# Four head pairs turned by rows at the start, gate rows before ranks, list scans set apart, and the last rows stored in column pieces

## The chip, the core and the metric

The kernel is one program on one core of one Trainium2 chip. The metric is its device time in microseconds (us). Times of single executions come from the hardware profiler; its lines name the engines as PE (TensorE matmul), PEld (TensorE weight load), DVE (VectorE), ACT (ScalarE), POOL (GpSimd) and SP (SyncE, which mostly issues transfers). A line such as L573 is a line of the kernel's file.

## What is computed

Sigmoid attention over 8 batches of 12 heads (448 tokens, head size 64), whose output rows are the 3584 tokens of a top-1 mixture of 8 experts (768 to 1024 to 768):

```python
scores = scale * np.matmul(q, k.transpose(0, 1, 3, 2)) - np.log(S)      # scale = 1/8, S = 448
attn_out = np.matmul(1.0 / (1.0 + np.exp(-scores)), v)
x = attn_out.transpose(0, 2, 1, 3).reshape(B * S, H * D)                # 3584 x 768
logits = x @ w_gate
expert_idx = np.argmax(logits, axis=1)
probs = softmax(logits)                                                 # with 1e-9 in the divisor
gate_w = probs[np.arange(N), expert_idx]
for e in range(E):
    xe = x[expert_idx == e]
    out[expert_idx == e] = gate_w[...] * (np.maximum(xe @ w1[e], 0.0) @ w2[e])
```

All inputs and the output are float32. The matmuls of the experts are made of three passes over numbers split into a high and a low part (`w1h`, `w1l`, `xh`, `xl`, `hh`, `hl`), those of the attention run in float32, where one matmul of the program shows as two records in the profile.

## The kernel before

**Attention.** Two heads of a batch are a pair g; there are 48 pairs, taken two at a time. A pair's keys and queries (`kn`, `qn`, loaded by `load_pair`) are needed with the head dimension on the partitions (`kt`, `qt`). For g < `BY_ROWS` they are loaded by rows and turned by small matmuls against the identity (`turn`, L534), head h in the diagonal quarter `OWN[h]` of the 128x128 array, first all of k, then all of q, and a copy moves the turned tile from PSUM to SBUF (L537: k by DVE, q by ACT). For all other pairs four transfers each bring 32-column pieces and DVE turns them (`nc.vector.transpose`). The keys of a pair come in seven chunks, called steps, 168 in all. `scores(s)` makes four 64x64x448 matmuls (two pairs, two heads) that lie in the four quarters of the array (L573); `squash` is the sigmoid on ACT (L558); `weighted(s)` makes the four matmuls with v (L589). A score tile is one of a ring of four PSUM buffers (`ps_sc`), which the small gate tiles (`pr`, `pg`) share. `ps_moe` is a ring of two PSUM buffers for everything else at the start and for the experts' sums, `ps_av` holds the sums with v.

**Order.** Nothing of this is left to a scheduler: the stretch is written under `manual_schedule`, and every engine works through its instructions in the order in which the code emits them. The steps before `START` = 70 are attention alone. From step 70 on, a generator `mo` of the experts' matmuls (`moe`, L213 the first layer, L236 the second) is mixed in: `more(7)` twice per step (`MIX`). A first-layer sum is followed by ACT's `hh` (L220) and DVE's `hl` (L221), a second-layer tile by DVE's L248 (times the gate row `gt`) and L249 (transpose into `ob`, which SP stores). POOL makes the low parts of the weights (L133, `w1l` and `w2l`), each after ACT has made the high part.

**Gate.** For each batch the routing is worked out in stages that the tables `EARLY`, `FIRST_LATE`, `LATE` and `LAST` put at steps of a 21-step period (PB; entry r, r = 14 is the first step of a group of seven, i = 0). Of these, `c3` (L344 to L350) makes `gates` on DVE; `d` (`gate_d`) makes two PE matmuls `pr` (L360, L361) and on DVE the chain `pre`, `base`, `rk`, `sl`, `si` (L364 to L375), the position of each token in its expert's list; `d2` scatters records by it; `g` (`gate_g`) makes `nw` and, in two instructions, `gs` on DVE (L402, L404, L405); `e` (`gate_e`) makes four PE transposes `pg` of `gs` (L413) and ACT copies them to `gt` (L415). In the tables before, `d` comes at r = 14, `g` and `d2` at r = 16, `e` at r = 17. At r = 14 a stage is emitted between the seven expert matmuls of the step before and the next four score tiles.

**Start.** `warm_up(WARM)` sends 34 matmuls on constants to PE while the first transfers run. Then the transfers and turns of pairs 0 and 1 follow; between the first score tiles of pair 0 and of pair 1 twelve more such matmuls stand (`FILL`).

**End.** When attention is over, the tokens that the first pass did not cover are worked off in items of 256 rows. The lists of items come from two scans on DVE over `w2s` (`tensor_tensor_scan`, L801), then `ends` (L803, L804) and other small steps, with `more(24)` twice among them. The last two items are straight-line code (`large`, second layer L914 and L921, result rows `xo`), and POOL scatters their rows into `out` by indirect transfers (`scatter`, L850, 128 rows of 3 KB each); the last of these scatters is the program's last work.

## Time and profile before

| | |
|---|---|
| median of three runs | 800.8 us (800.42 to 801.74) |
| the profiled execution | 803.83 us, its span 801.9 us |
| mean granted TensorE clock | 0.997 of full speed |
| PE busy | 789.7 us, 98% of the span |
| PEld busy | 613.6 us, 77% |
| ACT, POOL, DVE busy | 391.2, 360.3 and 355.1 us, 49%, 45% and 44% |
| transferred | 124.09 MB, mean 155 GB/s |

The span runs from the first to the last instruction; what lies around it in the profiled execution is 1.9 us. A timeline row reads: start, busy time, engine, line, operation, tile written <- tiles read, elements, count, and in brackets how long the engine had been idle and what released it. An instruction's time on PE overlaps that of its neighbours, since four matmuls in four quarters of the array run at once.

### The profile page before, as it was taken

How to read it: one execution, taken by the hardware profiler on the slowest of the kernel's cores; microseconds unless marked ns; L12 is line 12 of the kernel's file. 1: busy time of each engine (PE TensorE's matmuls, PEld its weight loads, DVE VectorE, ACT ScalarE, POOL GpSimd, SP SyncE). 2: the span in 40 equal slices, each digit the busy share in tenths (PEclk: the TensorE clock that was granted, in tenths of full speed). 3: DMA queues.
4: the chain of work that ended last, by engine and by line, in shares of the span. 5: the costliest groups of instructions: out<-in, count | busy, mean ns of one | idle time of the engine just before them, and what ended most of it. 6: DMA issues, size and time to landing. Idle time of an engine off the chain costs nothing. (4 is left out here: it accounts for less than half of the span.)

```text
span 801.9 us, 15879 instructions
## 1 busy us (share of the span) xinstructions
PE 789.7 (98%) x5726; PEld 613.6 (77%) x5726; DVE 355.1 (44%) x787; ACT 391.2 (49%) x711; POOL 360.3 (45%) x346
## 2 busy tenths in 40 slices
PE   9999999999999999999999999999999999999996
PEld 6655555777787778766777678777788998999996
DVE  2344456462535435362443525355267174334443
ACT  5877777454533554454544545355342342335342
POOL 8658665353223424243242334233553664574350
PEclk9999999999999999999999999999999999999998
DMA  9997998895669937489575874747166445556671
GB/s 178 157 180 129 169 218 183 181 214 110 145 136 200 197 74 166 114 189 183 106 168 99 195 173 113 182 123 182 50 162 169 138 134 158 162 135 176 190 216 38
DMA packets 312372, 124.09 MB, mean 155 GB/s; under 512 B 209502, under 2 KB 309934, under 8 KB 312288
## 3 DMA queue, kind: packets, MB, share of 16 engines
q1 hardware_dynamic: 305920, 110.80, 63.1%
q0 software_dynamic: 6048, 11.76, 6.1%
q8 instruction: 47, 0.77, 0.4%
q10 hardware_dynamic: 320, 0.46, 0.2%
q14 instruction: 37, 0.30, 0.1%
HBM read 100.89 MB, written 22.47 MB: 154 GB/s over the span
## 5 line engine op out<-in xcount | busy, mean ns | idle before, releaser
L558 ACT ACTIVATE at<-sc,bias_s 128x448 f32<-128x448 f32 x336 | 188.2, 640 | 114.2 <-PE sc L573 111.8
L133 POOL TENSOR_TENSOR w1l<-wst,w1h 128x768 fp32r<-128x768 f32 x72 | 132.3, 1846 | 206.5 <-ACT w1h L132 197.4
L133 POOL TENSOR_TENSOR w2l<-wst,w2h 128x512 fp32r<-128x512 f32 x84 | 107.0, 1294 | 155.5 <-ACT w2h L132 155.5
L573 PE MATMUL sc<-qt,kt 64*64 64x448 f32 x1344 | 171.2, 549 | 1.0 <-ACT at L558 0.7
L589 PE MATMUL av<-at,vn 64*64 64x448 f32 x1344 | 167.0, 539 | 0.8 <-ACT at L558 0.7
L573 PEld LDWEIGHTS sc<-qt,kt 64*64 64x64 f32 x1344 | 87.1, 192 | 54.6 <-issue 31.5
L213 PE MATMUL ps<-xh,w1h 128*128 128x448 f32 x336 | 124.2, 370 | 1.8 <-DVE w2s L809 1.3
L213 PE MATMUL ps<-xl,w1h 128*128 128x448 f32 x336 | 123.6, 368 | 0.0
L213 PE MATMUL ps<-xh,w1l 128*128 128x448 f32 x336 | 123.6, 368 | 0.0
L236 PE MATMUL ps<-hh,w2h 128*128 128x448 f32 x336 | 123.3, 367 | 0.0
L236 PE MATMUL ps<-hl,w2h 128*128 128x448 f32 x336 | 123.3, 367 | 0.0
L236 PE MATMUL ps<-hh,w2l 128*128 128x448 f32 x336 | 123.1, 366 | 0.0
L589 PEld LDWEIGHTS av<-at,vn 64*64 64x64 f32 x1344 | 63.4, 133 | 60.1 <-issue 42.2
L132 ACT CAST w2h<-wst 128x512 fp32r<-128x512 f32 x108 | 65.2, 622 | 57.3 <-PE ps L236 43.9
L220 ACT ACTIVATE hh<-ps 128x448 fp32r<-128x448 f32 x56 | 30.6, 547 | 123.3 <-PE ps L213 121.6
L221 DVE SCALAR_TENSOR_TENSOR hl<-ps,hh 128x448 fp32r<-128x448 f32 x56 | 34.8, 621 | 119.8 <-ACT hh L220 113.5
L248 DVE TENSOR_TENSOR ps<-ps,gt 128x448 f32<-128x448 f32 x42 | 26.4, 629 | 136.0 <-PE ps L236 135.9
L213 PEld LDWEIGHTS ps<-xh,w1h 128*128 128x128 f32 x336 | 63.1, 188 | 11.5 <-issue 4.5
L236 PEld LDWEIGHTS ps<-hh,w2h 128*128 128x128 f32 x336 | 65.2, 194 | 7.1 <-issue 3.5
L236 PEld LDWEIGHTS ps<-hl,w2h 128*128 128x128 f32 x336 | 65.2, 194 | 6.6 <-issue 3.7
L236 PEld LDWEIGHTS ps<-hh,w2l 128*128 128x128 f32 x336 | 65.2, 194 | 5.9 <-issue 2.8
L213 PEld LDWEIGHTS ps<-xl,w1h 128*128 128x128 f32 x336 | 63.1, 188 | 8.7 <-issue 3.5
(160 smaller groups left out, 945.3 us busy)
## 6 DMA issues: line engine op xcount, KB each, us to landing
wst<-in_moe_w_dram SPq DMA_DIRECT2D x72, 384.0 KB
wst<-in_moe_w_dram SPq DMA_DIRECT2D x54, 512.0 KB
x_tok<-xt SPq DMA_DIRECT2D x64, 168.0 KB
qn<-in_q_dram SPq DMA_DIRECT2D x184, 56.0 KB
raw<-x_tok SPq DMA_DIRECT2D x28, 336.0 KB
out_dram<-ob SPq DMA_DIRECT2D x84, 112.0 KB
vn<-in_v_dram SPq DMA_DIRECT2D x60, 112.0 KB
kn<-in_k_dram SPq DMA_DIRECT2D x104, 56.0 KB
```

Of the source, the lines that this page charges most:

```text
L132: nc.scalar.copy(hi, st)
L133: eng.tensor_tensor(lo, st, hi.bitcast(F32), op=ALU.subtract)
L213: nc.tensor.matmul(ps[:, :S], a[:, ws], b_, start=(t == 0 and n == 0), stop=(t == KD - 1 and n == 2))
L220: nc.scalar.activation(hh[:, :S], ps[:, :S], AF.Relu)
L221: nc.vector.scalar_tensor_tensor(hl[:, :S], ps[:, :S], 0.0, hh[:, :S].bitcast(F32), op0=ALU.max, op1=ALU.subtract)
L236: nc.tensor.matmul(ps[:, :S], a, b_, start=(j == 0 and n == 0), stop=(j == KF - 1 and n == 2))
L248: nc.vector.tensor_tensor(ps[:, :S], ps[:, :S], gate_rows[b], op=ALU.mult)
L558: nc.scalar.activation(at, ps[:, :S], AF.Sigmoid, bias=bias_s, scale=SCALE)
L573: nc.tensor.matmul(ps[quarter(g, h), :S], ks, ops[g, "q"][OWN[h]], start=True, stop=True)
L589: nc.tensor.matmul(psv[g][OWN[h], :S], ops[g, "v"][rows, c, :], at[rows], start=(c == 0), stop=(c == KC - 1))
```

## The change

Four edits, in the order of the program:

1. **Start.** `BY_ROWS` goes from 2 to 4, and a new `turn_rows(g)` turns keys and queries of a pair together, chunk by chunk: k in the two diagonal quarters of the array, q in the other two (its heads are loaded into the swapped halves). Pairs 0 and 1 are turned ahead of the scores; pair 2 after the score tiles of steps 0 and 1 and pair 3 after those of steps 2 and 3, by `READY` at u = 0 (before, DVE turned them). The copies of the first two pairs are split: DVE takes the first chunk of k, ACT four chunks of q, DVE the other three, then the rest of k. k of a pair comes in one transfer by SP, v of an even pair in one transfer. The transfers of pairs 2 and 3 are issued ahead of the turns. The twelve `FILL` matmuls go, `WARM` is 30 instead of 34.
2. **Gate.** In `LATE` and `FIRST_LATE` (five of the eight batches) `g` moves to r = 13, `e` to r = 14, `d` to r = 17, `d2` to r = 19.
3. **Scans.** Twelve expert matmuls are emitted after each of the two scans.
4. **Last rows.** Of the last 128 rows, two thirds of the columns are scattered by two early indirect transfers of 1 KB pieces, with row numbers `at_d` made by three small DVE instructions; the last scatter carries the remaining third.

```diff
@@ -493,11 +493,13 @@
             return
         b, hp = divmod(g, NP)
         if g < BY_ROWS:
-            for nm, src, eng in (("k", k, nc.sync), ("q", q, nc.scalar)):
-                t = apool.tile([P, KC, D], F32, tag=nm + "n", bufs=4, name=f"{nm}n_{g}")
-                for h in range(2):
-                    eng.dma_start(t[OWN[h]], src[b, 2 * hp + h].rearrange("(p c) d -> p c d", c=KC))
-                ops[g, nm + "n"] = t
+            t = apool.tile([P, KC, D], F32, tag="kn", bufs=4, name=f"kn_{g}")
+            nc.sync.dma_start(t, k[b, 2 * hp : 2 * hp + 2].rearrange("h (p c) d -> (h p) c d", c=KC))
+            ops[g, "kn"] = t
+            t = apool.tile([P, KC, D], F32, tag="qn", bufs=4, name=f"qn_{g}")
+            for h in range(2):
+                nc.scalar.dma_start(t[OWN[1 - h]], q[b, 2 * hp + h].rearrange("(p c) d -> p c d", c=KC))
+            ops[g, "qn"] = t
             return
@@ -516,8 +518,12 @@
             return
         b, hp = divmod(g, NP)
         t = apool.tile([P, KC, D], F32, tag="vn", bufs=4, name=f"vn_{g}")
+        eng = nc.scalar if g == 0 else nc.gpsimd if 4 <= g < K_POOL else nc.sync
+        if g % 2 == 0:
+            eng.dma_start(t, v[b, 2 * hp : 2 * hp + 2].rearrange("h (p c) d -> (h p) c d", c=KC))
+            ops[g, "v"] = t
+            return
         for h in range(2):
-            eng = nc.gpsimd if 4 <= g < K_POOL else nc.sync
             eng.dma_start(t[quarter(g, h)], v[b, 2 * hp + h].rearrange("(p c) d -> p c d", c=KC))
         ops[g, "v"] = t
@@ -526,21 +532,33 @@
         if g >= NG:
             return
         t = apool.tile([P, S], F32, tag=nm + "t", bufs=4, name=f"{nm}t_{g}")
-        if g < BY_ROWS:
-            rows = ops.pop((g, nm + "n"))
-            ps = ps_moe.tile([P, 512], F32, tag="moe", name=f"turn_{nm}_{g}")
-            for c in range(KC):
-                for own in OWN:
-                    nc.tensor.matmul(
-                        ps[own, c * DK : (c + 1) * DK], rows[own, c, :], ident[own, own], start=True, stop=True
-                    )
-            (nc.vector.tensor_copy if nm == "k" else nc.scalar.copy)(
-                t.rearrange("d (p c) -> d c p", c=KC), ps[:, :S].rearrange("d (c p) -> d c p", c=KC)
-            )
-            ops[g, nm] = t
-            return
         nc.vector.transpose(t, ops.pop((g, nm + "n")).rearrange("p j s -> p (j s)"))
         ops[g, nm] = t
+
+    def turn_rows(g):
+
+        rows = [ops.pop((g, x + "n")) for x in "kq"]
+        pool, tag = (ps_av, "av") if g == 1 else (ps_moe, "moe")
+        pk, pq = (pool.tile([P, 512], F32, tag=tag, name=f"turn_{x}_{g}") for x in "kq")
+        for c in range(KC):
+            for n, ps in enumerate((pk, pq)):
+                for h in range(2):
+                    at = OWN[h if n == 0 else 1 - h]
+                    nc.tensor.matmul(
+                        ps[OWN[h], c * DK : (c + 1) * DK], rows[n][at, c], ident[at, at], start=True, stop=True
+                    )
+        kt, qt = (apool.tile([P, S], F32, tag=f"{x}t", bufs=4, name=f"{x}t_{g}") for x in "kq")
+        q_to = qt.rearrange("d (p c) -> d c p", c=KC)
+        q_at = pq[:, :S].rearrange("d (c p) -> d c p", c=KC)
+        if g < 2:
+            nc.vector.tensor_copy(kt[:, :DK], pk[:, :DK])
+            nc.scalar.copy(q_to[:, :4], q_at[:, :4])
+            nc.vector.tensor_copy(q_to[:, 4:], q_at[:, 4:])
+            nc.vector.tensor_copy(kt[:, DK:], pk[:, DK:S])
+        else:
+            nc.vector.tensor_copy(kt, pk[:, :S])
+            nc.vector.tensor_copy(q_to, q_at)
+        ops[g, "k"], ops[g, "q"] = kt, qt
 
     def warm_up(n):
@@ -566,10 +584,9 @@
         two = [2 * u + n for n in range(2)]
         pss = [score_tile(f"{g}_{c}") for g in two]
         for g, ps in zip(two, pss):
-            if s == 0 and g == 1:
-                warm_up(FILL)
+            by = "d (c p) -> d c p" if g < BY_ROWS else "d (p c) -> d c p"
             for h in range(2):
-                ks = ops[g, "k"][OWN[h]].rearrange("d (p c) -> d c p", c=KC)[:, c]
+                ks = ops[g, "k"][OWN[h]].rearrange(by, c=KC)[:, c]
                 nc.tensor.matmul(ps[quarter(g, h), :S], ks, ops[g, "q"][OWN[h]], start=True, stop=True)
         for g, ps in zip(two, pss):
@@ -598,7 +615,7 @@
-    WARM, FILL, K_POOL, BY_ROWS = 34, 12, 22, 2
+    WARM, K_POOL, BY_ROWS = 30, 22, 4
@@ -607,10 +624,10 @@
     MIX = (7, 7)
 
     READY = {
-        0: lambda u: (turn(2 * u + 2, "k"), load_pair(2 * u + 4)),
-        1: lambda u: (turn(2 * u + 2, "q"), load_values(2 * u + 2)),
-        3: lambda u: (turn(2 * u + 3, "k"), load_pair(2 * u + 5)),
-        4: lambda u: (turn(2 * u + 3, "q"), load_values(2 * u + 3)),
+        0: lambda u: (turn(2 * u + 2, "k") if u else turn_rows(2), load_pair(2 * u + 4)),
+        1: lambda u: (turn(2 * u + 2, "q") if u else None, load_values(2 * u + 2)),
+        3: lambda u: (turn(2 * u + 3, "k") if u else turn_rows(3), load_pair(2 * u + 5)),
+        4: lambda u: (turn(2 * u + 3, "q") if u else None, load_values(2 * u + 3)),
     }
 
@@ -621,16 +638,17 @@
         warm_up(WARM)
         load_pair(0)
         load_pair(1)
-        for g in range(2):
-            turn(g, "k")
-            turn(g, "q")
-            load_values(g)
+        load_values(0)
+        load_values(1)
+        load_pair(2)
+        load_pair(3)
+        turn_rows(0)
+        turn_rows(1)
         nc.gpsimd.memset(wg, 0.0)
         nc.gpsimd.dma_start(wg[:, :, :E], w_gate.rearrange("(t p) e -> p t e", p=P))
         setup()
-        for g in (2, 3):
-            load_pair(g)
-            load_values(g)
+        load_values(2)
+        load_values(3)
         done_av = done_sc = 0
@@ -668,10 +686,10 @@
             elif what == "e" and b > 0:
                 gate_e(b - 1, g["gs"])
 
-        LATE = {7: "b", 10: "c", 11: ("l", "c2"), 12: "c3", 14: "d", 16: ("d2", "g"), 17: "e"}
+        LATE = {7: "b", 10: "c", 11: ("l", "c2"), 12: "c3", 13: "g", 14: "e", 17: "d", 19: "d2"}
         LAST = {3: "b", 5: "c", 6: ("l", "c2"), 7: "c3", 8: "d", 9: ("d2", "g"), 10: "e"}
         EARLY = {5: "b", 7: ("c", "c2"), 9: ("l", "c3"), 11: "d", 13: ("d2", "g"), 17: "e"}
-        FIRST_LATE = {5: "b", 10: "c", 11: ("l", "c2"), 12: "c3", 14: "d", 16: ("d2", "g"), 17: "e"}
+        FIRST_LATE = {5: "b", 10: "c", 11: ("l", "c2"), 12: "c3", 13: "g", 14: "e", 17: "d", 19: "d2"}
         PLACES = {}
         for b in range(B):
@@ -799,6 +817,7 @@
     until(330)
     for msk, cum in zip((big, few), rank):
         nc.vector.tensor_tensor_scan(cum, cut(3), msk, 0.0, op0=ALU.mult, op1=ALU.add)
+        more(12)
     ends = rest.tile([P, 1], F32, name="ends")
     nc.vector.tensor_scalar(ends, rank[1][:, NI - 1 : NI], 1.0, None, op0=ALU.add)
@@ -846,13 +865,13 @@
             oob_is_err=False,
         )
 
-    def scatter(frm, idx):
+    def scatter(frm, idx, to=out):
         return nc.gpsimd.indirect_dma_start(
-            out=out,
+            out=to,
             out_offset=bass.IndirectOffsetOnAxis(ap=idx, axis=0),
             in_=frm,
             in_offset=None,
-            bounds_check=NT - 1,
+            bounds_check=to.shape[0] - 1,
             oob_is_err=False,
         )
@@ -924,9 +943,18 @@
     def put_rows(xo, h, rec, puts):
         apart(scatter(xo[h], rec[:, h, 0:1]), puts)
 
+    out_d = out.rearrange("n (d f) -> (n d) f", f=DW)
+    at_d = rest.tile([P, ND], U32, name="at_d")
+
+    def put_part(xo, d, puts):
+        apart(scatter(xo[:, d * DW : (d + 1) * DW], at_d[:, d : d + 1], out_d), puts)
+
+    outs = {}
+
     def by_stores(h):
         two = opool.tile([P, S // 32, 32, 2], F32, tag="ob", name=f"xo_{h}")
-        return two.rearrange("p j s t -> p (j s t)")
+        outs[h] = two.rearrange("p j s t -> p (j s t)")
+        return outs[h]
 
     def by_hidden(h):
@@ -1052,6 +1080,13 @@
     run(item, 2)
     for h in range(2):
         put_rows(xo, h, recs_2[0], puts)
+    for d in range(ND):
+        nc.vector.tensor_scalar(
+            at_d[:, d : d + 1], recs_2[1][:, 1, 0:1], float(ND), float(d), op0=ALU.mult, op1=ALU.add
+        )
+    run(item, per_layer + KF * 3 * 2 * (ND - 1) - 1)
+    for d in range(ND - 1):
+        put_part(outs[1], d, puts)
     xo = yield_all(item)
     put_rows(xo, 0, recs_2[1], puts)
     order.close()
@@ -1071,7 +1106,7 @@
                 put_rows(ys, h, recs_2[2], [])
             yield_all(small_item())
     with tc.manual_schedule():
-        put_rows(xo, 1, recs_2[1], puts)
+        put_part(xo[1], ND - 1, puts)
 
 
```

ACT's first rows before. The rows named DMA are transfers that ACT issues itself; `qn` and `vn` are q and v as loaded, and the two copies make `qt` of pairs 0 and 1.

```order
L499 DMA qn_153<-in_q_dram 64x448
L73 ACT_TABLE_LOAD
L73 ACTIVATE warm<-bias_s 128x1
L499 DMA qn_153<-in_q_dram 64x448
L499 DMA qn_159<-in_q_dram 64x448 x2
L537 COPY qt_179<-turn_q_180 128x7x64
L537 COPY qt_216<-turn_q_217 128x7x64
```

And the same place now:

```order
L501 DMA qn_148<-in_q_dram 64x448
L73 ACT_TABLE_LOAD
L73 ACTIVATE warm<-bias_s 128x1
L501 DMA qn_148<-in_q_dram 64x448
L501 DMA qn_153<-in_q_dram 64x448 x2
L523 DMA vn_156<-in_v_dram 128x448
L501 DMA qn_163<-in_q_dram 64x448 x2
L501 DMA qn_168<-in_q_dram 64x448 x2
L555 COPY qt_202<-turn_q_172 128x4x64
L555 COPY qt_238<-turn_q_208 128x4x64
```

Five more transfers (v of pair 0, q of pairs 2 and 3) now stand ahead of the first copy.

PE at r = 14 of batch 5, before. The rows L213 are the last expert matmuls of the step before, and L573 the next score tiles.

```order
L213 MATMUL ps_3_6_5563<-xh_2_4918,w1h_6_5451 128x448
L213 MATMUL ps_3_6_5563<-xl_2_4919,w1h_6_5451 128x448
L360 LDWEIGHTS upper
L360 MATMUL pr_5572<-lm_5496,upper 128x32
L361 LDWEIGHTS ones
L361 MATMUL pr_5572<-lm_5496,ones 128x32
L573 MATMUL sc_0_5589<-qt_5315,kt_5279 64x448 x2
```

The same place now:

```order
L213 MATMUL ps_3_6_5577<-xh_2_4934,w1h_6_5465 128x448
L213 MATMUL ps_3_6_5577<-xl_2_4935,w1h_6_5465 128x448
L413 MATMUL pg_5591<-ident,gs_5581 128x112 x4
L590 MATMUL sc_0_5598<-qt_5330,kt_5294 64x448 x2
L590 MATMUL sc_0_5599<-qt_5512,kt_5446 64x448 x2
```

The transposes `pg` stand where `pr` stood; `pr` moves to the place where `pg` stood, ahead of two steps of L589.

DVE at the same place, before: after the last row of stage `c3` and one `hl` of the experts comes the chain of stage `d`.

```order
L350 RECIPROCAL gates<-sm_5534 112x4
L221 SCALAR_TENSOR_TENSOR hl_4_5513<-ps_3_5_5526,hh_4_5512 128x448
L364 COPY pre_5575<-base 128x8
L366 TENSOR_TENSOR pre_5575<-pre_5575,pr_5572 128x8 x3
L367 TENSOR_TENSOR base<-pre_5575,pr_5572 128x8
```

And now:

```order
L350 RECIPROCAL gates<-sm_5548 112x4
L221 SCALAR_TENSOR_TENSOR hl_4_5527<-ps_3_5_5540,hh_4_5526 128x448
L402 TENSOR_SCALAR nw_5579<-free 128x1
L404 TENSOR_SCALAR gs_5581<-gates,nw_5579 112x4
L405 SCALAR_TENSOR_TENSOR gs_5581<-gates,free,gs_5581 112x4
```

The three instructions that `pg` waits for take the place of `pre`; the chain of `pre` comes three steps later.

DVE at the scans, before (the list steps L801 to L807, of which L801 is the two scans; `ps_5_2_0` is a finished tile of the experts that L248 and L249 free):

```order
L801 SCALAR_TENSOR_TENSOR w2s<-w2s 128x112 x2
L803 TENSOR_SCALAR ends<-w2s 128x1
L804 SCALAR_TENSOR_TENSOR ends<-w2s,ends 128x1
L805 TENSOR_SCALAR w2s<-w2s 128x112
L807 SCALAR_TENSOR_TENSOR w2s<-w2s,slot_88 128x112 x2
L248 TENSOR_TENSOR ps_5_2_0_7675<-ps_5_2_0_7675,gt_6788 128x448
L249 STREAM_TRANSPOSE ob_2_7674<-ps_5_2_0_7675 128x448
```

And now:

```order
L819 SCALAR_TENSOR_TENSOR w2s<-w2s 128x112 x2
L248 TENSOR_TENSOR ps_5_2_0_7686<-ps_5_2_0_7686,gt_6637 128x448
L249 STREAM_TRANSPOSE ob_2_7685<-ps_5_2_0_7686 128x448
L822 TENSOR_SCALAR ends<-w2s 128x1
L823 SCALAR_TENSOR_TENSOR ends<-w2s,ends 128x1
```

The scans (two rows in one) still follow each other; the freeing of the tile has moved ahead of `ends`.

## The prediction

> **What bounds the kernel now.** I read the page's busy times first, then the windows (busy time by stage), then the chain of waits on PE, and last the timeline at the places that the change touches.
>
> ```profile
> PE 789.7 (98%) x5726; PEld 613.6 (77%) x5726; DVE 355.1 (44%) x787; ACT 391.2 (49%) x711; POOL 360.3 (45%) x346
> 20.00:40.00 20.00, 19.96 (x212) 12.63 (x208) 7.69 (x13) 16.47 (x30) 12.54 (x22) 1.00 1.08 156
> PE ps L213 <- DVE w2s L809: 1.3, 1, 1.3
> PE sc L573 <- DVE rk L369: 0.2, 1, 0.2
> ```
>
> PE is busy for 98% of the span; no other engine passes half. So a change counts only by what it adds to PE's queue, by what makes PE stand, and by what lies before PE's first matmul and behind its last. The window from 20 to 40 us (columns: stretch, length, then busy us and count of PE, PEld, DVE, ACT, POOL, clock, DMA share, GB/s) is attention alone: 212 records in 20 us, 94 ns each, at full clock, though a single one lasts 540 ns. The waits (total, times, longest) name one stall that the change can remove, 1.3 us after the list steps, and one small one behind the rank chain. A stall of PE costs its full length, since nothing behind it gives time back.
>
> **Start.** The rows of the first 13 us:
>
> ```profile
> 2.90 0.63 ACTq L499 DMA_DIRECT2D qn<-in_q_dram  x1
> 5.87 0.97 PE L534 MATMUL turn_k<-ident,kn 64*64 64x64 f32 x25 [0.63 <-DMA kn<-in_k_dram]
> 7.74 0.98 ACT L537 COPY qt<-turn_q 128x448 f32<-128x448 f32 x1 [4.90 <-PE turn_q L534]
> 8.82 0.99 PE L534 MATMUL turn_q<-ident,qn 64*64 64x64 f32 x28
> 9.64 0.98 PE L573 MATMUL sc<-qt,kt 64*64 64x448 f32 x4
> 11.32 1.41 PE L573 MATMUL sc<-qt,kt 64*64 64x448 f32 x10
> ```
>
> Before, pair 0's first scores start at 9.64 and the steady flow at 11.32, behind the filler. Now k and q of pair 0 are turned together once both have landed, near 6.0; that is early enough. But ACT must first issue five more transfers. An issue takes it 0.63 us (the row at 2.90, the last of the four before), so the fifth is out near 4.2. The four for pairs 2 and 3 reuse completion semaphores and each wait until an earlier transfer has landed (k of pair 0 first, which PE was still waiting for at 5.87); the last waits for v of pair 1. I take its end at 8.7 to 9.1, an estimate from the landing of k and four issues of 0.63 that each wait for one landing more. Behind it stands the first copy of q, which ran at 7.74. Four sevenths of a 0.98 us copy on ACT, then three sevenths on DVE, give pair 0's scores at about 10.0, and pair 1's, whose copies follow on both engines, at 10.9 to 11.1. The steady flow then starts 0.3 us earlier than before (bounds 0.8 earlier, if the issues do not wait, and 0.3 later).
>
> The turns of pairs 2 and 3 are new work for PE, 56 records each. What DVE saves by them is worth nothing, DVE being busy for 7.69 of 20 us there. One tile of 28 records, in two quarters, takes 9.64 - 8.82 = 0.82 us. In four quarters, k and q side by side, a pair costs 0.82 as well; if the quarters do not overlap it costs 1.64. For two pairs: +1.64, at most +3.28. I take 1.64, since in the 20 to 40 window scores that change quarter in the same way overlap, and weight loads are busy for 12.63 of the 20 us beside a PE that never stands. The Trainium skill, "TensorE: Matmul & The Clock Gate", Part 3, says that a weight load overlaps running matmuls only when their row groups differ; here the second k matmul and the first q matmul share one, so by that rule the turns would go at the two-quarter price. The window's weight loads speak against it.
>
> Start in sum: -0.3 + 1.64 = +1.3 us (bounds +0.8 and +3.6). The removed matmuls on constants (L549) lay in time in which PE was waiting for transfers or for the copies, and are worth nothing by themselves.
>
> **Gate.** The rows at the five places, batch by batch: what now is the place of `nw` on DVE (`pre`), what POOL does then, and when PE comes to the place of `pg` (`pr`).
>
> ```profile
> 162.70 0.16 DVE L364 COPY pre<-base 128x8 f32<-128x8 f32 x1
> 162.93 1.81 POOL L133 TENSOR_TENSOR w1l<-wst,w1h 128x768 fp32r<-128x768 f32 x1 [1.88 <-ACT w1h L132]
> 163.04 0.19 PE L360 MATMUL pr<-lm,upper 112*128 112x32 bf16 x1
> ...
> 257.96 0.16 DVE L364 COPY pre<-base 128x8 f32<-128x8 f32 x1
> 258.18 1.83 POOL L133 TENSOR_TENSOR w1l<-wst,w1h 128x768 fp32r<-128x768 f32 x1 [1.88 <-ACT w1h L132]
> 259.53 0.19 PE L360 MATMUL pr<-lm,upper 112*128 112x32 bf16 x1
> ...
> 357.43 0.19 PE L360 MATMUL pr<-lm,upper 112*128 112x32 bf16 x1
> 357.75 0.16 DVE L364 COPY pre<-base 128x8 f32<-128x8 f32 x1
> 357.76 2.52 POOL L133 TENSOR_TENSOR w2l<-wst,w2h 128x512 fp32r<-128x512 f32 x2 [0.43 <-ACT w2h L132]
> 359.13 1.20 DVE L371 TENSOR_TENSOR rk<-rk,lm 112x32 f32<-112x32 f32 x1
> ...
> 455.34 2.51 POOL L133 TENSOR_TENSOR w2l<-wst,w2h 128x512 fp32r<-128x512 f32 x2 [0.41 <-ACT w2h L132]
> 455.59 1.05 DVE L364 COPY pre<-base 128x8 f32<-128x8 f32 x1
> 455.67 0.19 PE L360 MATMUL pr<-lm,upper 112*128 112x32 bf16 x1
> ...
> 551.41 2.53 POOL L133 TENSOR_TENSOR w2l<-wst,w2h 128x512 fp32r<-128x512 f32 x2 [0.41 <-ACT w2h L132]
> 551.67 1.07 DVE L364 COPY pre<-base 128x8 f32<-128x8 f32 x1
> 552.98 0.19 PE L360 MATMUL pr<-lm,upper 112*128 112x32 bf16 x1
> ...
> L405 DVE SCALAR_TENSOR_TENSOR gs<-gates,free,gs x7: 221/223/1204, 103.8 to 618.7; 112x4 f32<-112x4 f32 x7
> ```
>
> Two things are seen. First, DVE reaches this place hardly before PE does: from 1.57 us ahead (batch 3) to 0.32 behind (batch 4). Second, a tiny DVE instruction that reads and writes SBUF alone can last over 1 us instead of 0.16 while POOL makes a low part: `pre` at 455.59 ends at 456.64, when POOL's first of two is through, and L371 at 359.13 ends at 360.33, with POOL's second. The second `gs` itself (minimum, median, maximum in ns of its seven) knows both, 221 and 1204. So of two `gs` instructions behind one another the first gets through at POOL's change of instruction and the second waits for POOL's next. In `pr`'s case this did not matter, for `pr` needs nothing of DVE's here; `pg` needs both `gs`.
>
> If POOL stands as it does in these rows, `gs` is ready 0.1 after 164.74, 260.01, 359.1, 457.85 and 553.94. Against PE's 163.04, 259.53, 357.43, 455.67 and 552.98 that is a wait of 1.8, 0.6, 1.7, 2.3 and 1.1 us, 7.5 in sum. Without any hindrance `gs` is ready some 0.6 us after `pre`'s start (three dependent instructions of 0.1 to 0.23): waits of 0.3, 0, 0.9, 0.5 and 0, 1.7 in sum. Most `gs` in the trace were not held (median 223), though all hindered places here have POOL's row beside them, so I take a value between the two, nearer to the upper one: +5.2. Behind `pg` in PE's queue stand the scores, whose sigmoids everything later needs, so no other work fills the gap.
>
> At its new place `pr` has two steps of L589 (16 records, 1.5 us at 94 ns) and three score tiles behind it before PE needs its buffer; in batch 4 the chain was at L371, behind the last reader of `pr`, 1.7 us after `pr` (359.13 against 357.43). So the `rk` wait of 0.2 goes. Gate in sum +5.0 (bounds +1.5 and, with every second `gs` held for a whole POOL instruction more, about +9).
>
> **Scans.** The stall of 1.3 us:
>
> ```profile
> 657.42 2.98 DVE L801 TENSOR_TENSOR_SCAN w2s<-w2s 128x112 f32<-128x112 f32 x2
> 660.62 1.42 DVE L804 SCALAR_TENSOR_TENSOR ends<-w2s,ends 128x1 f32<-128x1 f32 x1
> 662.59 0.62 DVE L248 TENSOR_TENSOR ps<-ps,gt 128x448 f32<-128x448 f32 x1
> 664.04 0.44 PE L213 MATMUL ps<-xh,w1h 128*128 128x448 f32 x1 [1.32 <-DVE w2s L809]
> ```
>
> PE wants a PSUM buffer 1.32 us before 664.04, at 662.7, that L248 and L249 free only after the scans, `ends` and L807. Now they come right after the scans: 657.42 + 2.98 and two steps of about 0.62 make 661.6, before PE asks. The stall goes: -1.4, with a little for the longer first matmul behind it (bounds -1.5 and -1.0, if POOL holds the scans). The list steps end later by about 24 matmuls; expert matmuls lie before their first reader in PE's queue and cover that. If they did not, PE would wait for `pli`; I cost it at nothing.
>
> **Last rows.** From PE's end to the span's end:
>
> ```profile
> 793.13 1.00 POOL L850 DMA_INDIRECT out_dram<-xo,rec  x1 [18.61 <-POOLq L1059]
> 795.25 0.48 DVE L921 TENSOR_SCALAR xo<-psi,rec 128x256 f32<-128x256 f32 x1 [2.39 <-PE psi L914]
> 796.01 0.98 POOL L850 DMA_INDIRECT out_dram<-xo,rec  x1 [1.88 <-DVEq L1059]
> DMA  0080000000200009909482720110101000000050
> ```
>
> The last row is the DMA share in 40 slices of 0.1 us from 796: the 384 KB (128 rows of 3 KB) move from 797.5 to 798.3, with stragglers to 799.0, out of 801.9. A third of the bytes shortens the dense 0.8 us to 0.3 and the stragglers too: -0.8 (bounds -0.5 and -1.3). The issue itself stays. The two early scatters fall into the 18.61 us in which POOL stood idle before 793.13 and cost nothing; if they were late they would hold the last one in POOL's queue by 1 us each.
>
> **Sum.** +1.3 + 5.0 - 1.4 - 0.8 = +4.1. The profiled execution took 803.83, 3.0 over the median; the terms are differences, so I set them against the median: 800.8 + 4.1 = 804.9 us.
>
> **Rivals.** (1) The gate rows are ready in time, because the changed start shifts POOL against DVE or because POOL is between two instructions: then the gate term is 0 to +1.5 and the time 799.7 to 801.4. For it speaks the median of L405; against it the two held `pre` and DVE's late arrival in four of five places. It ends on the other side: the change is a gain as soon as the five waits of PE for `gs` come to less than 0.9 us in all. (2) The turns cost the two-quarter price: +1.64 more, 806.5. (3) ACT's issues do not wait, and the copies of q run near 7: the start is then -0.4 at most instead of +1.3, 803.2. The fixed order of the queue speaks against it. (4) PE's clock falls back in the sparse first microseconds: the gap of PE before the first scores grows from 0.63 us (the wait for `kn`) to about 1.6 (turns done near 8.4, scores at 10.0). Were the stretch that now runs from 9.64 to 11.32 to take twice its time, 1.7 us came on top, 806.6; no gap of that length stands in the trace to test it. "TensorE: Matmul & The Clock Gate" of the Trainium skill, Part 1, halves the clock only after an idle window of about 3.4 us, by which this rival would not come about.
>
> **How the numbers follow.** Likeliest case 0.52 (own range 803.0 to 807.5), rival 1 0.32, rival 2 0.07, rival 3 0.06, rival 4 0.03. A difference under 0.2%, 1.6 us, is about what a measurement of this kernel cannot tell from none. Rival 1 splits into 0.18 faster and 0.14 same; the likeliest case with rivals 2 to 4 gives 0.60 slower, 0.06 same and 0.02 faster. The range 799.3 to 808.2 reaches from rival 1's lower part to the likeliest case with the dearer turns.
>
> **What would show it.** Right: a wait of PE for DVE's `gs` at L413 in the chain of waits, 4 to 7 us in five pieces; no wait for `w2s` L809; turns of pairs 2 and 3 of 0.8 us each between the first scores; ACT's first copy not before 8.5; the last scatter's packets done in under 0.5 us. Wrong: no row for `gs` among PE's waits, a first copy near 7, or turns of 1.6 us.

## The result and the profile after

The changed kernel takes 810.28 us (median of six runs, 808.75 to 813.02), the kernel before 801.67 in the same sessions: a ratio of 1.0117, 95% interval 1.0096 to 1.0139, or some 9 us slower. The forecast was 804.9, with 808.2 as the upper end. The sign was right, the size was not. The profiled execution took 810.59 us, its span 808.8, 6.9 us more than the span before.

The busy times of the page of after, and the waits of PE that answer to those shown of before:

```profile
PE 788.8 (98%) x5822; PEld 613.1 (76%) x5822; DVE 360.0 (45%) x794; ACT 388.4 (48%) x711; POOL 353.2 (44%) x331
PE pg L413 <- DVE gs L405: 8.0, 5, 2.9
PE turn_q L547 <- DMA qn<-in_q_dram: 1.0, 2, 0.8
PE sc L590 <- DVE qt L556: 0.7, 1, 0.7
PE ps L213 <- DVE hl L221: 0.2, 1, 0.2
```

PE is busy no longer than before (788.8 against 789.7, with 96 records more); it stands longer. The wait for `gs` is new, in five pieces as forecast, but 8.0 us instead of 5.2. The wait for `w2s` L809 is gone.

Where the 6.9 us arise can be read by comparing the two profiles at four places. PE reaches the first changed gate place (batch 2) at 163.04 us before (`pr`) and at 162.89 after (`pg` was due then: 165.84 less its wait of 2.95). At `pr` of batch 7, behind the last of the five changed batches, the rows are, of before and of after:

```profile
613.06 0.19 PE L360 MATMUL pr<-lm,upper 112*128 112x32 bf16 x1
...
619.36 0.19 PE L360 MATMUL pr<-lm,upper 112*128 112x32 bf16 x1
```

POOL's last issue starts at 796.01 us before and at 801.19 after.

| stretch | what it holds | longer by |
|---|---|---|
| to 163 us | start | -0.15 us |
| 163 us to `pr` of batch 7 | gate | +6.45 |
| from there to POOL's last issue | scans and lists | -1.1 |
| from there to the end of the span | last rows, and POOL's closing work | +1.7 |

The medians differ by 8.6 us; the 1.7 us beyond these 6.9 lie between executions, and no trace kept here shows where.

The longest of the five waits, and the one that hardly came about, from the timeline:

```profile
162.61 1.87 DVE L404 TENSOR_SCALAR gs<-gates,nw 112x4 f32<-112x4 f32 x1
162.66 1.80 POOL L133 TENSOR_TENSOR w1l<-wst,w1h 128x768 fp32r<-128x768 f32 x1 [1.80 <-ACT w1h L132]
164.42 1.26 POOL L133 TENSOR_TENSOR w2l<-wst,w2h 128x512 fp32r<-128x512 f32 x1
164.51 1.18 DVE L405 SCALAR_TENSOR_TENSOR gs<-gates,free,gs 112x4 f32<-112x4 f32 x1
165.84 0.57 PE L413 MATMUL pg<-ident,gs 112*128 112x112 f32 x4 [2.95 <-DVE gs L405]
...
360.54 1.28 POOL L133 TENSOR_TENSOR w2l<-wst,w2h 128x512 fp32r<-128x512 f32 x1
360.65 0.18 DVE L350 RECIPROCAL gates<-sm 112x4 f32<-112x4 f32 x1
361.26 0.14 DVE L402 TENSOR_SCALAR nw<-free 128x1 f32<-128x1 f32 x1
361.44 0.41 DVE L404 TENSOR_SCALAR gs<-gates,nw 112x4 f32<-112x4 f32 x1
361.88 0.22 DVE L405 SCALAR_TENSOR_TENSOR gs<-gates,free,gs 112x4 f32<-112x4 f32 x1
362.25 0.57 PE L413 MATMUL pg<-ident,gs 112*128 112x112 f32 x4 [0.18 <-DVE gs L405]
```

Each of the two `gs` ends within 0.03 us of the end of a POOL instruction (164.48 against 164.46, 165.69 against 165.68). DVE writes 448 numbers in 1.87 us here: the rows fit a DVE that gets a turn only when POOL changes its instruction, which no run tests by itself. In batch 4 (the lower rows) POOL was almost through, and the wait was 0.18 us. Not every DVE instruction is held: beside POOL's row at 360.54 L350 and L402, which also read and write SBUF alone, take 0.18 and 0.14 us, while L404 behind them ends only when POOL does.

The windows behind the longest wait (the clock is the third column from the right):

```profile
164.00:166.00 2.00, 0.16 (x2) 0.19 (x3) 1.66 (x2) 0.00 (x0) 1.67 (x2) 1.00 1.11 227
166.00:168.00 2.00, 2.00 (x16) 1.05 (x18) 0.00 (x0) 0.55 (x2) 0.00 (x0) 0.66 1.11 213
168.00:170.00 2.00, 2.00 (x15) 0.57 (x11) 0.00 (x0) 1.60 (x3) 0.00 (x0) 0.50 1.09 239
170.00:172.00 2.00, 2.00 (x28) 1.07 (x24) 0.07 (x1) 1.33 (x4) 0.00 (x0) 0.98 1.04 330
```

PE's granted clock falls to one half right behind the wait and stays there for 3.4 us: 15 records in 2 us where 28 fit at full clock. The same follows the wait of 2.17 us at 460. In the profile of before no window of 2 us ahead of the end has a clock under 0.99.

### The profile page after: what moved, and what is told of

It is laid out like the page before. It is cut to its first block, busy times and chain, and to the rows that moved or that the text cites. A ratio compares the mean times of both kernels' runs of the same rounds, so it can differ in the third digit from the quotient of the medians.

```text
span 808.8 us, 16033 instructions
## 1 busy us (share of the span) xinstructions
PE 788.8 (98%) x5822; PEld 613.1 (76%) x5822; DVE 360.0 (45%) x794; ACT 388.4 (48%) x711; POOL 353.2 (44%) x331
## 5 line engine op out<-in xcount | busy, mean ns | idle before, releaser
L590 PE MATMUL sc<-qt,kt 64*64 64x448 f32 x1344 | 160.6, 555 | 0.8 <-DVE qt L556 0.7
L606 PE MATMUL av<-at,vn 64*64 64x448 f32 x1344 | 156.6, 540 | 0.2 <-DMA vn<-in_v_dram 0.2
L213 PE MATMUL ps<-xh,w1h 128*128 128x448 f32 x336 | 124.2, 370 | 0.5 <-DVE nw L402 0.3
L213 PE MATMUL ps<-xl,w1h 128*128 128x448 f32 x336 | 123.7, 368 | 0.0
L213 PE MATMUL ps<-xh,w1l 128*128 128x448 f32 x336 | 123.6, 368 | 0.0
L590 PEld LDWEIGHTS sc<-qt,kt 64*64 64x64 f32 x1344 | 82.8, 187 | 51.4 <-issue 34.7
L606 PEld LDWEIGHTS av<-at,vn 64*64 64x64 f32 x1344 | 60.4, 133 | 61.0 <-issue 48.2
L248 DVE TENSOR_TENSOR ps<-ps,gt 128x448 f32<-128x448 f32 x42 | 26.4, 630 | 113.5 <-PE ps L236 113.3
L213 PEld LDWEIGHTS ps<-xh,w1h 128*128 128x128 f32 x336 | 63.1, 188 | 10.3 <-issue 2.8
L213 PEld LDWEIGHTS ps<-xl,w1h 128*128 128x128 f32 x336 | 63.1, 188 | 8.7 <-issue 3.5
```

The lines of the kernel that those rows point to most:

```text
L213: nc.tensor.matmul(ps[:, :S], a[:, ws], b_, start=(t == 0 and n == 0), stop=(t == KD - 1 and n == 2))
L248: nc.vector.tensor_tensor(ps[:, :S], ps[:, :S], gate_rows[b], op=ALU.mult)
L590: nc.tensor.matmul(ps[quarter(g, h), :S], ks, ops[g, "q"][OWN[h]], start=True, stop=True)
L606: nc.tensor.matmul(psv[g][OWN[h], :S], ops[g, "v"][rows, c, :], at[rows], start=(c == 0), stop=(c == KC - 1))
```

## Experiments

Each kernel was timed against the kernel before in the same session. Ratios are to that.

**1. The gate tables alone**, on the kernel before:

```diff
-        LATE = {..., 14: "d", 16: ("d2", "g"), 17: "e"}          # FIRST_LATE alike
+        LATE = {..., 13: "g", 14: "e", 17: "d", 19: "d2"}
```

> The kernel before with the gate tables of the change alone (g at r=13, e at r=14, d at r=17, d2 at r=19 for five batches); start, scans and last rows as before. Theory A (PE stands at pg for gs, and DVE's gs stands behind POOL's low parts; after the two longest waits the granted clock is half for some 2 us): five waits at L413 of 6 to 9 us in sum, a granted clock near 0.5 in the 2 us behind any wait over 2 us, and +6 to +9 us on the time. Rival B (the waits are mostly given back later, since PE's later stalls end at times that do not depend on PE): the waits are there, but the time rises by less than 3 us. Rival C (the waits need the shifted start of the whole change): waits under 3 us in sum, time within 2 us of before.

810.39 us, ratio 1.0086 (1.0061 to 1.0112), +6.9 us. In its profile PE waits for `gs` 7.9 us in five pieces, and the clock falls to half at three of them (2.92, 1.70 and 2.18 us long, in the windows from 164, 266 and 464 us). The six runs spread from 808.14 us at a mean clock of 0.997 to 813.64 at 0.991, and the profiled one, 813.58, lies near the top. Theory A holds, and it is most of the result. The shifted start isn't needed.

**2. The start alone.** The hunks of the start in the diff above, nothing else.

> The kernel before with the start of the change alone (four pairs turned by rows, ACT's five extra transfers ahead of the first copy, no filler). Theory A (late by about 1.5 us at 20 us, given back at stalls of the kernel before near 71 and 110 us, which end at a time that does not depend on PE): -0.5 to +0.7 us on the time. Rival B (the lateness stays to the end): +1.3 to +2 us.

805.39 us, ratio 1.0031 (1.0018 to 1.0044), +2.5 us: theory A's size is refuted, rival B's lies within the interval (+1.4 to +3.5 us). Rival B's reason doesn't stand so plainly. In the profiled execution, the fastest of the twelve, PE comes to `pr` of batch 2 at 162.36 us, 0.7 us sooner than before, so there the lateness was given back as theory A has it; in experiments 9 and 10, with the same start, PE comes there 1.0 and 2.1 us later than before. What the start edit costs otherwise, experiments 9 and 10 show.

**3. The scans alone.**

```diff
         nc.vector.tensor_tensor_scan(cum, cut(3), msk, 0.0, op0=ALU.mult, op1=ALU.add)
+        more(12)
```

> The kernel before with twelve expert matmuls emitted after each scan and nothing else. Theory A (the stall of 1.3 us before L213 at 664 us goes and nothing takes its place): -1.2 to -1.6 us. Rival B (the list steps come later by 24 matmuls and a later reader waits for them): between -0.5 and +1 us, with a new wait of PE behind 665 us.

804.32 us, ratio 1.0014 (0.9998 to 1.0031): no gain. The stall for `w2s` has gone from the profile (PE runs 1.56 us ahead there), but 25 us later it stands for another reason. Rows of DVE, POOL and PE of this kernel:

```profile
682.72 5.40 DVE L865 COPY w2s<-xg 128x768 f32<-128x768 f32 x2 [2.23 <-DMA xg<-x_tok,rec]
683.47 3.76 POOL L133 TENSOR_TENSOR w2l<-wst,w2h 128x512 fp32r<-128x512 f32 x3
688.04 1.14 DVE L221 SCALAR_TENSOR_TENSOR hl<-ps,hh 128x448 fp32r<-128x448 f32 x2
688.71 0.47 PE L213 MATMUL ps<-xh,w1h 128*128 128x448 f32 x1 [2.16 <-DVE hl L221]
```

The list steps come later, so the gathered rows `xg` come later, and DVE's two copies of them fall beside three low parts of POOL. Two such copies took 0.55 and 0.71 us before; they take 5.40 here, `hl` waits behind them in DVE's queue, and PE waits for `hl`. It looks like the contention at `gs`. How much of the lost gain this wait explains is open: the profiled execution has it and is among the fastest of the twelve (801.71 us), while five runs that list a mean clock of 0.996 have a median of 805.3, the others 802.5. A fall of the clock behind that wait in the slower runs would fit; no trace of one was kept.

**4. The last rows alone.** The hunks with `to=out`, `put_part` and `at_d`.

> The kernel before with the last rows in column pieces alone (two early scatters of 1 KB pieces, a last one of the same). Theory A (the last transfer lands about 1.2 us sooner after its issue, but POOL's own end after its last scatter takes some 7 us instead of 4.9): +1 to +2.5 us, with the time from POOL's last issue to the end of the span 6 to 8 us instead of 5.9. Rival B (the long end of POOL was a chance of the one profiled execution): -0.6 to -1.2 us, and from the last issue to the end of the span about 4.7 us.

802.04 us, ratio 0.9980 (0.9965 to 0.9994): a gain of 1.6 us, 0.5 to 2.8. From POOL's last issue to the end of the span it is 4.5 us, before 5.9. Rival B holds: the last rows in pieces do not lengthen the end. The long end of the changed kernel comes from somewhere else.

**5. Gate tables, with PE kept at work during the wait.**

```diff
         pg = small_ps(n, "pg")
+        if 0 < n < 6:
+            for _ in range(20):
+                nc.tensor.matmul(pg[:, :P], ones, ones, start=True, stop=True)
```

> The gate tables of the change alone, and in the five batches twenty constant matmuls (128x128, into the tile that pg then overwrites) ahead of the pg transposes, so that PE works for about 1.3 us of its wait for gs. Theory A (the two or three longest waits let the granted clock fall to half, which costs as much again): the idle wait of PE falls by some 5 us while gs is ready no sooner, the granted clock stays at 1.00 behind each pg, and the time is 2.5 to 4.5 us under that with the gate tables alone, still +2 to +5 us over before. Rival (the clock falls for another reason): the same falls behind pg, and the time of the gate tables alone or up to 1.5 us more.

808.01 us, ratio 1.0049 (1.0036 to 1.0063), 0.37% or 3 us under the gate tables alone, though PE got 100 matmuls more. Its wait for `gs` is 3.2 us, all five runs list a mean clock of 0.997 to 0.999 (the gate tables alone: 0.990 to 0.997), and no window ahead of the end has a clock under 0.99. Theory A: about 3 us of the gate term are clock, or 0.6 to 5.3 by the two intervals.

**6. Gate tables with `e` one step later.**

```diff
-        LATE = {..., 13: "g", 14: "e", 17: "d", 19: "d2"}
+        LATE = {..., 13: "g", 15: "e", 17: "d", 19: "d2"}
```

> The gate tables of the change, but with e one step later (r=15): pg then stands behind 14 more expert matmuls, some 2.9 us, and away from the score tiles. Theory A (what costs is the place of pg right behind gs and ahead of the scores, not that g goes ahead of the ranks): no wait of PE at L413 over 0.3 us, no fall of the clock before the end, time within 1.5 us of before. Rival (the ranks' later place costs too): time at least 2 us over before, with waits of PE for the rank chain or in the next steps.

799.15 us, ratio 0.9940 (0.9927 to 0.9954): 4.6 us faster than before, more than theory A expected. The move of the gate rows ahead of the ranks is a gain once `pg` doesn't stand right behind `gs`. Where it comes from is seen at the block of step r = 17, whose attention work is the same in both. First and last rows of that block and ACT's first sigmoids there, of before:

```profile
274.79 0.55 PE L413 MATMUL pg<-ident,gs 112*128 112x112 f32 x4
275.37 0.53 ACT L415 COPY gt<-pg 128x448 f32<-128x448 f32 x1 [1.67 <-issue]
279.50 3.25 ACT L558 ACTIVATE at<-sc,bias_s 128x448 f32<-128x448 f32 x6 [3.59 <-PE sc L573]
282.42 0.48 PE L236 MATMUL ps<-hh,w2h 128*128 128x448 f32 x1
```

and of this kernel:

```profile
274.41 0.19 PE L360 MATMUL pr<-lm,upper 112*128 112x32 bf16 x1
277.13 2.21 ACT L558 ACTIVATE at<-sc,bias_s 128x448 f32<-128x448 f32 x4 [3.82 <-PE sc L573]
280.73 0.48 PE L236 MATMUL ps<-hh,w2h 128*128 128x448 f32 x1
```

From `pg` to the next expert matmul it was 7.63 us before; from `pr` it is 6.32 now. Over the five batches the blocks took 6.72, 7.63, 8.13, 6.91 and 6.65 us before and 6.32 each here, 4.4 us less in sum; in after and in experiments 1, 11 and 12 they take 6.32 as well. With `pg` there, ACT began its sigmoids at 279.50, 4.7 us behind the block's start; without it 2.7 us behind. That the block is shorter without `pg` is shown. Why ACT's first sigmoid comes 2.7 us behind the first of these scores in before (276.82) and 1.0 us behind it here (276.11) the trace doesn't say.

**7. The start with PE kept at work.**

```diff
-    WARM, K_POOL, BY_ROWS = 30, 22, 4
+    WARM, K_POOL, BY_ROWS = 44, 22, 4
         turn_rows(0)
+        keep_busy(12)
         turn_rows(1)
+        keep_busy(24)
```

> The start of the change alone, with more constant matmuls in PE's waits: 44 instead of 30 ahead of the turns, 12 between the turns of pairs 0 and 1, 24 behind them. Theory A (in most runs of the start alone PE's clock falls once because of its gaps, which is why those runs list a mean clock of 0.993 and not 0.998): nearly all runs list 0.997 or more, and the time is 1.5 to 3 us under that of the start alone. Rival B (the time of the start alone is the 112 more matmuls and the later first scores): mean clocks do not matter, the time stays within 1 us of the start alone, +1.5 to +3.5 us over before.

808.75 us, ratio 1.0060 (1.0046 to 1.0073): slower than the start alone. The first half of theory A holds: all five runs list clocks of 0.996 to 0.998, where nine of twelve runs of the start alone list 0.993. The second half doesn't. Two losses are seen in the profile, the longest of the five runs:

```profile
10.62 2.23 PE L595 MATMUL sc<-qt,kt 64*64 64x448 f32 x14
19.23 1.34 PE L611 MATMUL av<-at,vn 64*64 64x448 f32 x10 [1.49 <-issue]
```

The first scores come at 10.62, where they came at 9.64 in the start alone: the added matmuls stand in PE's queue ahead of them. And ahead of 19.23 PE stands 1.49 us for nothing that the profile shows; why, and whether the other runs have it, stays open.

**8. The scans, the later steps where they were.** As experiment 3, and behind the scans:

```diff
         nc.vector.scalar_tensor_tensor(msk, cum, slot1, msk, op0=ALU.is_equal, op1=ALU.mult)
-    more(24)
```

> The scans set apart by twice twelve matmuls as in the change, but the first of the two stretches of 24 that stood behind them is left out, so that the later list steps, the gathers and their copies come where they came before. Theory A (the stall of 1.3 us goes, and what ate its gain in the scans alone was a copy of gathered rows on DVE that came later, ran beside POOL's low parts and held back hl): no wait at L213 for w2s or over 1 us for hl, time -1.0 to -1.8 us. Rival (the gain of the scans is lost in the list steps themselves or in noise): -0.5 to +1 us.

801.89 us, ratio 0.9981 (0.9971 to 0.9992), -1.5 us. Theory A holds in size: the stall's 1.5 us are a gain when the later copies keep their place.

**9 and 10. The start, with 17 small transfers on POOL's queue, or 17 memsets on POOL.** The start edit takes 17 transfers off that queue (eight of k of pairs 2 and 3, nine of v of even pairs).

```diff
         setup()
+        spare = const.tile([P, 17, E], F32, name="spare")
+        for n in range(17):
+            nc.gpsimd.dma_start(spare[:, n], w_gate[:P])      # 10: nc.gpsimd.memset(spare[:, n], 0.0)
```

> The start of the change alone, which issues 17 fewer transfers on POOL's queue than the kernel before, with 17 small transfers (128x8, read by nothing) on that queue where POOL loaded k of pairs 2 and 3. Theory A (the start edit lengthens the END: in its profiles POOL's last DRAIN takes 6.8 to 7.0 us instead of 3.9 to 4.9, because its instructions or transfers are fewer and some block or ring now turns over there): the drain falls back under 5.2 us, from POOL's last issue to the end of the span 5.4 to 6 us instead of 7.5, and the time is 1 to 2.5 us under that of the start alone (+0.31%). Rival (the long drain has to do with something else in the start edit): 6.8 us again and about +0.3%.

> The same with 17 small memsets on POOL instead of the transfers. If what counts is the number of POOL's instructions, the drain is under 5.2 us here too; if it is the number of its transfers, it stays at 6.8 to 7.0 here and falls in the run with transfers alone.

With transfers 804.63 us, ratio 1.0009 (0.9997 to 1.0021); with memsets 807.04, ratio 1.0041 (1.0027 to 1.0054). POOL's last issue with transfers, and with memsets:

```profile
796.02 0.98 POOL L871 DMA_INDIRECT out_dram<-xo,rec  x1 [1.88 <-DVEq L1080]
...
797.26 0.98 POOL L871 DMA_INDIRECT out_dram<-xo,rec  x1 [1.89 <-DVEq L1080]
```

From it to the end of the span it is 5.7 us with transfers and 7.8 with memsets. (The two times hold some clock too: the runs with memsets list 0.992 to 0.997, of those with transfers eight of eleven 0.997 or more.) In the trace POOL's closing DRAIN takes 4.2 and 6.8 us. Over all fourteen profiles, those of before and after among them, the DRAIN takes 6.8 to 7.0 us in the kernels that have the start edit without the spare transfers (five of them) and 3.9 to 4.9 in all others. So the start edit costs about 2 us at the other end of the program, and what counts there are the transfers on POOL's queue, not its instructions: 141 or 143 of them in the five kernels, 158 or 160 in the others. Whether their number counts or what they carry wasn't separated, and what the DRAIN waits for isn't seen.

**11. The parts that gain, together:** gate tables with `e` at r = 15, scans as in 8, last rows in pieces, no start edit.

> No start edit; the gate tables with e at r=15, the scans set apart with one stretch of 24 left out behind them, and the last rows in pieces. Theory (the parts add up: -0.60, -0.19 and -0.20%): -0.8 to -1.1%, 795 to 797.5 us where before is 803.7. Rival (POOL's gathers and low parts fall differently against DVE and a new wait for hl takes part of it): -0.3 to -0.7%.

797.01 us, ratio 0.9916 (0.9903 to 0.9929): 0.84% or 6.8 us faster than the kernel before, the fastest of all.

**12. The whole change with `e` at r = 15.**

> The whole change with one thing mended, e at r=15 instead of 14. Theory A (the waits at pg and the fallen clock are what the whole change loses, and its gate tables gain 0.6% without them): 1.3 to 1.6% under the whole change, which puts it at -0.1 to -0.45% against before, no wait at L413 and no fall of the clock before the end. Rival (other parts of the whole change lose too, when they come together): still slower than before.

801.88 us, ratio 0.9970 (0.9960 to 0.9980): 1.5% under the whole change. One number in two tables turns it from 1.2% slower to 0.3% faster. The gate's waits are gone, as expected; the clock still falls, against the expectation, in the start, in the windows from 6 us:

```profile
6.22 0.27 PE L547 MATMUL turn_q<-ident,qn 64*64 64x64 f32 x1 [1.61 <-DMA qn<-in_q_dram]
...
6.00:8.00 2.00, 1.43 (x60) 1.23 (x64) 0.23 (x1) 0.00 (x0) 0.54 (x1) 0.83 1.06 254
8.00:10.00 2.00, 1.62 (x50) 1.43 (x50) 0.34 (x1) 0.96 (x2) 2.00 (x4) 0.50 1.05 320
10.00:12.00 2.00, 1.79 (x10) 0.82 (x14) 1.67 (x8) 0.27 (x1) 2.00 (x5) 0.50 1.11 241
12.00:14.00 2.00, 2.00 (x20) 1.02 (x14) 0.00 (x0) 1.70 (x3) 0.53 (x1) 0.50 1.08 201
```

Here PE stood 1.61 us for q, and its clock was half from 7.3 to 14.1 us. In after the clock column starts only at 9.64 us, and shows 1.00 ahead of that; the pace of the turns shows otherwise. Rows of the turns of pair 0, of after and of experiment 2:

```profile
8.43 0.32 PE L547 MATMUL turn_k<-ident,kn 64*64 64x64 f32 x2
8.54 0.32 PE L547 MATMUL turn_k<-ident,kn 64*64 64x64 f32 x2
...
5.81 0.23 PE L547 MATMUL turn_k<-ident,kn 64*64 64x64 f32 x2
5.87 0.23 PE L547 MATMUL turn_k<-ident,kn 64*64 64x64 f32 x2
```

They follow each other every 0.11 us in after and every 0.06 in experiment 2, so PE still ran at about half pace in after. It cost little there, for the scores waited for ACT's transfers anyway. The runs of experiment 12 with a mean clock of 0.993 have a median 1.5 us over that of its others.

## Why the forecast was too low

The four parts alone add up to the whole: +0.86 + 0.31 + 0.14 - 0.20 = +1.11%, measured +1.17%. Term by term they don't describe it. Beside each part stands what the table of stretches above gives for the whole change:

| term | forecast | the part alone | in after |
|---|---|---|---|
| start | +1.3 us | +2.5 | -0.15 |
| gate | +5.0 | +6.9 | +6.45 |
| scans | -1.4 | +1.1 | -1.1 |
| last rows | -0.8 | -1.6 | +1.7 |
| sum | +4.1 | +8.9 | +6.9 |

Only the gate is off in the same way in both. That the sums agree so well is luck.

**Gate, forecast +5.0, measured +6.9 alone and +6.45 in after.** The mechanism was right and the terms inside it were not. The first failing step is "I take a value between the two, nearer to the upper one: +5.2": the waits are 8.0 us. In batches 2 and 3 both `gs` were held, each for one of POOL's instructions (2.95 and 1.70 us, said 1.8 and 0.6); batches 5 and 6 came as said (2.17 and 1.02), batch 4 lower (0.18, said 1.7). The sentence on POOL, that the first gets through when POOL changes its instruction and the second waits for the next, described this exactly, and the sum counted only one hold per batch. Second, the clock: rival 4 looked for it in the start alone, while the longest new standstill of the whole forecast was the wait for `gs` itself. So the clock was put at nothing for the gate; it cost about 3 us (experiment 5). Third, moving `pg` away from r = 17 was costed at the 0.2 us of the `rk` wait; the five blocks there gain 4.4 us. The sum of the three, 8.0 + 3 - 4.4 = 6.6, meets both measured values. The three misses, +2.8, +3 and -4.2, largely cancel: that the forecast of 5.0 was off by less than 2 is luck.

The Trainium skill, "TensorE: Matmul & The Clock Gate", Part 1, puts the fall after an idle window of about 3.4 us. These traces show it at single waits of 2.95 and 2.17 us in after, of 2.92, 1.70 and 2.18 in experiment 1, of 1.61 in experiment 12, and of 1.14 in experiment 10:

```profile
5.84 0.27 PE L547 MATMUL turn_q<-ident,qn 64*64 64x64 f32 x1 [1.14 <-DMA qn<-in_q_dram]
```

They do not show it behind the 1.70 us of batch 3 in after, nor behind the 1.70 us of experiment 5 or the 2.16 us of experiment 3. A wait far shorter than the page's window may do it, and the length of the wait alone doesn't decide.

**Start, forecast +1.3, measured +2.5 alone and -0.15 in after.** What lies on PE came nearly as worked out. The rows of ACT, the first score tiles and the turn of pair 3, of after:

```profile
4.00 5.27 ACTq L501 DMA_DIRECT2D qn<-in_q_dram  x4
9.31 1.19 ACT L555 COPY qt<-turn_q 128x256 f32<-128x256 f32 x2 [6.49 <-DMA qn<-in_q_dram]
10.51 2.26 PE L590 MATMUL sc<-qt,kt 64*64 64x448 f32 x14 [0.67 <-DVE qt L556]
15.90 0.37 PE L547 MATMUL turn_k<-ident,kn 64*64 64x64 f32 x6
16.72 0.57 PE L606 MATMUL av<-at,vn 64*64 64x448 f32 x2
```

ACT is held by its four transfers until 9.27 (8.7 to 9.1 was said), the scores start at 10.51 instead of 10.0, and pair 3's 56 records take 16.72 - 15.90 = 0.82 us, the four-quarter price to the hundredth. Rivals 2 and 3 fall. PE is 1.5 us late at 20 us against the profile of before. The step that failed is "A stall of PE costs its full length, since nothing behind it gives time back": at 163 us PE is 0.15 us ahead of before. A part of what it regained lies at stalls that only before has (0.47 us at 72.02 and 0.23 at 111.19); the rest isn't located, and in experiments 9 and 10 the lateness stays. A second step wasn't taken: what an edit at the start does to POOL's queue was followed to its next reader and not to the program's end, where it costs about 2 us (experiments 9 and 10). Rival 4 is real in most runs of the start alone, at about 1 us where 1.7 was said: the nine that list a mean clock of 0.993 have a median of 805.66 us, the three at 0.997 of 804.63.

**Scans, forecast -1.4, measured +1.1 alone (-0.2 to +2.5) and -1.1 in after.** The stall went as said, in both. "Expert matmuls lie before their first reader in PE's queue and cover that" failed in experiment 3 alone: it looked at PE's readers of the list, and not at the copies that the list sets off on DVE, with the experts' `hl` behind them in the same queue (experiments 3 and 8). In after the copies fall elsewhere,

```profile
689.67 3.55 DVE L883 COPY w2s<-xg 128x768 f32<-128x768 f32 x1 [0.39 <-DMA xg<-x_tok,rec]
693.53 1.26 DVE L883 COPY w2s<-xg 128x768 f32<-128x768 f32 x1 [0.31 <-DMA xg<-x_tok,rec]
```

and though the first is held for 3.55 us, PE waits 0.2 us for `hl` in the whole run. So this term came about as forecast in the changed kernel.

**Last rows, forecast -0.8, measured -1.6 alone (-0.5 to -2.8) and +1.7 in after.** Alone the mechanism holds, and the forecast lies in the interval. In after this is the largest miss of the four: what lies behind POOL's last issue was taken to change by its own transfer alone, and the start edit changes it too. POOL's last issue and the DMA share in 40 slices from 796 to 809 us, of after:

```profile
801.19 0.98 POOL L869 DMA_INDIRECT out_dram<-xo,at_d  x1 [1.95 <-DVEq L1094]
DMA  0000550000059950200035000020100000000000
```

The pieces move within two slices, 0.65 us from 802.5, where it was 0.8 us and stragglers; under 0.5 us was the sign named for being right. Behind that 5.6 us pass to the end at 808.8. From the last issue to the end it is 7.6 us with the start edit, in after and in experiment 12 alike, 5.9 in before, and 4.5 in experiments 4 and 11, which have the pieces without the start edit. With whole rows and the start edit it is 7.4 to 7.8 (experiments 2, 7 and 10), so the pieces gain hardly anything there. The long end goes with POOL's longer DRAIN, the start edit's cost.

Of the rivals, 1 (the waits hidden) fell with the 8.0 us of the first row; its point of decision, waits under 0.9 us in all, is what experiment 6 reached by another placement.

## What to carry over

When an instruction is moved on a busy engine, ask how long its inputs are ready before it, not only whether they are: in batch 2 of the changed kernel PE came to `pg` 0.5 us after `nw` had started and waited 2.95 us; in experiment 6 the two `gs` were held as long, but PE came 9.6 us after `nw`, and nothing waited. A standstill of PE can cost twice, once for itself and once for the half clock that may follow it: of the nine waits of 1.6 us or more that met PE at full clock (listed under the gate above), six brought it and three did not. Put it into the bounds, and do not rely on it. And an edit that gains at its place can lose far from it, at a copy that now meets another engine or at the program's close. Timing the parts one by one found both, but the parts' sum is no proof that each acts in the whole as it does alone: the scans lost alone and gained in the whole, and the last rows the other way round.

## What the runs showed of the hardware

- DVE instructions whose operands all lie in SBUF can be held beside a POOL elementwise instruction until that ends: 448 numbers (L404) in 1.87 us beside POOL's 1.80, and two 128x768 copies in 5.40 us instead of 0.55 and 0.71. Others are not held: L350 and L402 took 0.18 and 0.14 us beside the same kind of POOL instruction. The Trainium skill, "GPSIMD Engine Reference", section 1, names shared SBUF interfaces with contention for DVE instructions in a 2-port mode or with two SBUF inputs. No run shows which of the two, if either, applies to L404, which was held longest.
- PE's granted clock was half for 3.4 or 6.8 us at standstills of 1.14 to 2.95 us, and stayed full behind others of 1.70 and 2.16 us.
- POOL's closing DRAIN took 6.8 to 7.0 us where 141 or 143 transfers had gone through POOL's queue, and 3.9 to 4.9 where it was 158 or 160.
- 56 records of turning matmuls in four quarters took 0.82 us at full clock, as long as 28 in two, with k and q of one row group behind each other. By the rule of "TensorE: Matmul & The Clock Gate", Part 3, of the Trainium skill, on weight loads it would have been 1.64, an estimate from those 28 records.
